# Zero rows of the short chunk on another engine, and the second pair's transposes and scores in other queues and banks

## The chip, the core and the metric

The kernel runs on one core of a Trainium2 chip. The metric is device time in microseconds, the median of several executions, and lower is better. One execution has been recorded by the hardware profiler, and all rows shown are from such recordings. The engines are TensorE (PE: matmuls; PEld: its weight loads), VectorE (DVE), ScalarE (ACT), GpSimd (POOL) and SyncE (SP, which issues nearly all transfers here). Each engine works through its own queue in program order. Matmuls write PSUM, which is divided into eight banks.

## The reference

Causal linear attention with a decay for each head ("retention"), followed by a gated feed-forward layer:

```python
# q, k, v: (8, 8, 576, 64) fp32
scores = (1 / sqrt(64)) * q @ k.T
gamma  = 1 - 2.0 ** (-5 - arange(8))                  # one for each head
D      = where(i >= j, gamma ** (i - j), 0)
x      = ((scores * D) @ v)                           # -> (4608 tokens, 512)
gate   = 1 / (1 + exp(-(x @ w_gate)))                 # w_gate, w_val: (512, 1536)
out    = (gate * (x @ w_val)) @ w_out                 # w_out: (1536, 512)
```

## The kernel before, in words

Each of the 8 sequences of 576 tokens is cut into chunks of 128, 128, 128, 128 and 64 tokens, which gives 45 steps; step 4 and step 9 are the short ones of 64 tokens ("short chunk") in the first two sequences. The decay is folded into q and k when they are cast to bf16 (tables qtab, ktab). Within a chunk the scores are masked by a triangle and multiplied with v; between chunks a state of k.T v is carried on for each head (PSUM tile "st", copied to "sbd" for each step). The attention's output goes, transposed, into xT. The feed-forward layer then takes blocks of tokens of xT: 12 GLU units (h: gate and value matmuls of 4 steps each, L567; a sigmoid on ACT; a product on VectorE) and the output matmuls ("op").

The order on every engine is written out by hand, in the order of the program text:

- The first four steps are done as two pairs (A = 0 and 1) of 256 tokens. For a pair, `cast_pair` casts and scales half of the heads of k, q or v (L232, v on ACT at L229), `pair_t` transposes half of k or q on TensorE into one PSUM bank and copies it out by the engine given (L297, L307), `pair_qk` makes half of the scores in two PSUM banks and masks them on VectorE (L316, L321), `pair_st` adds to the state (L330), `tile_sv` copies the state (L338), `pair_pv` makes the output (L352 from the state, L359 from the scores) and `pair_out` copies it to xT (L366).
- `fill(n)` issues n matmuls of zeros (L136) into a GLU bank; their result isn't used.
- `h_first(fcs, a, e)` runs GLU units of the first 512 tokens, for the given pieces of the hidden layer and columns. `cast_w` casts pieces of the GLU weights (L209), `cast_wo` those of the output weights (L214).
- Steps 4 to 9 run through `phase_tk`, `phase_tq`, `phase_qk`, `phase_st`, `phase_sv` and `phase_pv`, woven into the GLU and output matmuls of earlier tokens by `advance`. `run_phase("t", s)` first issues loads up to step s + 5 and casts up to step s + 2 (k, for later steps q, and v; on POOL). So when step 4 starts, POOL gets the casts of step 6 (L239, L258), which need the loads of step 6.
- In `phase_qk` a short chunk's scores fill 64 of the 128 partitions of tile "pte"; the other 64 are set to zero (L416), because `phase_pv` reads all 128 (L459).

PSUM banks by pool: "tr" 1, "qk" 2, "pv" 1, "st" 1, and "ffn" 3, which the GLU units, the fills, the output matmuls and some of the pairs' work share in turn. Loads go into 18 buffers, output rows into 4 ("osb"). The first output matmuls (L769) work on three blocks of 128 tokens at once and follow the product of step 4; the fourth block follows at L780.

Of the kernel before, what the change touches and what calls it, by code (L numbers as in the profile page):

```python
# [16 lines left out]
def kernel(  # L17
# [17 lines left out]
    nc = tc.nc  # L35
# [4 lines left out]
    P = 128  # L40
# [14 lines left out]
    tr_psum = ctx.enter_context(tc.tile_pool(name="tr_psum", bufs=1, space=PS))  # L55
    qk_psum = ctx.enter_context(tc.tile_pool(name="qk_psum", bufs=2, space=PS))
    pv_psum = ctx.enter_context(tc.tile_pool(name="pv_psum", bufs=1, space=PS))
    st_psum = ctx.enter_context(tc.tile_pool(name="st_psum", bufs=1, space=PS))
    ffn_psum = ctx.enter_context(tc.tile_pool(name="ffn_psum", bufs=3, space=PS))
# [71 lines left out]
    def fill(n):  # L131

        ps = ffn_psum.tile([P, 512], FP32, tag="ffn", name=f"idle_{fill.at}")
        fill.at += 1
        for i in range(n):
            nc.tensor.matmul(ps, lhsT=blank[:, 0:P], rhs=blank, start=True, stop=True)  # L136
# [69 lines left out]
    def cast_w(nm, f, nf, i, eng):  # L206
        r = NKC // nf
        at = (slice(None), slice(i * r, (i + 1) * r), slice(f * P, (f + nf) * P))
        eng(out=(wg_sb if nm == "g" else wv_sb)[at], in_=parts.pop((nm, f, i)))  # L209

    on_pool, on_act, on_dve = nc.gpsimd.tensor_copy, nc.scalar.copy, nc.vector.tensor_copy
# [75 lines left out]
    def half(x):  # L287
        return slice(x * 64, x * 64 + 64)
# [3 lines left out]
    def pair_t(nm, A, g, psum, tag, eng):  # L292
        ps = psum.tile([P, 2, 2, P], BF16, tag=tag, name=f"{nm}Tp_{A}_{g}")
        for i in range(2):
            for r in range(2):
                m = 2 * g + i
                nc.tensor.matmul(ps[:, i, r, :], lhsT=natural[nm, A][:, r, 2 * m:2 * m + 2, :], rhs=ident,  # L297
                                 is_transpose=True, start=(i == 0 and r == 0), stop=(i == 1 and r == 1))
        if nm == "k":
            if g == 0:  # L300
                turned["kp", A] = att_pool.tile([P, M, 2, P], BF16, tag="kp", name=f"kp_{A}", bufs=1)
            o = turned["kp", A][:, 2 * g:2 * g + 2]
        else:
            if g == 0:
                turned["qp", A] = att_pool.tile([P, M, 2 * P], BF16, tag="qp", name=f"qp_{A}", bufs=1)
            o = turned["qp", A][:, 2 * g:2 * g + 2, :].rearrange("p m (t r) -> p m r t", r=2)
        eng(out=o, in_=ps)  # L307

    def pair_qk(A, g, psum, tag):
        ps = [psum.tile([P, 2, 2, P], FP32, tag=tag, name=f"qkp_{A}_{g}_{hh}") for hh in range(2)]  # L310
        for i in range(2):
            m = 2 * g + i
            for r in range(2):
                for a in range(2):
                    for hh in range(2):
                        nc.tensor.matmul(ps[hh][half(a), i, r, :], lhsT=turned["kp", A][half(hh), m, r, half(a)],  # L316
                                         rhs=turned["qp", A][half(hh), m, a * P:(a + 1) * P], start=True, stop=True)
        if g == 0:
            probs["p", A] = att_pool.tile([P, 2, M, 2, P], BF16, tag="ptp", name=f"ptp_{A}", bufs=1)
        for hh in range(2):  # L320
            nc.vector.tensor_tensor(out=probs["p", A][:, hh, 2 * g:2 * g + 2], in0=ps[hh],  # L321
                                    in1=trip.unsqueeze(1).to_broadcast([P, 2, 2, P]), op=ALU.mult)
# [12 lines left out]
    def tile_sv(s, eng):  # L335
        sb = sbd[s % 3]
        for hh in range(2):
            eng(out=sb[half(hh), :, half(hh)], in_=st_tiles[STEPS[s][0]][half(hh)])  # L338
        state[s] = sb
# [3 lines left out]
    def pair_pv(A, g, a):  # L343
        s = 2 * A + a
        if g == 0:
            pair_ps[s] = (tr_psum if a else pv_psum).tile([P, M, P], FP32, tag="tr" if a else "pv", name=f"pvp_{s}")
        ps = pair_ps[s]
        if s > 0:
            for i in range(2):
                m = 2 * g + i  # L350
                for hh in range(2):
                    nc.tensor.matmul(ps[half(hh), m, :], lhsT=state[s - 1][:, m, half(hh)],  # L352
                                     rhs=turned["qp", A][:, m, a * P:(a + 1) * P],
                                     start=(m == 0), stop=False, skip_group_check=True)
        for i in range(2):
            m = 2 * g + i
            for r in range(2):
                for hh in range(2):
                    nc.tensor.matmul(ps[half(hh), m, :], lhsT=natural["v", A][half(a), r, 2 * m + hh, :],  # L359
                                     rhs=probs["p", A][half(a), hh, m, r, :],  # L360
                                     start=(s == 0 and m == 0 and r == 0), stop=(m == M - 1 and r == 1),
                                     skip_group_check=True)
# [39 lines left out]
    def phase_qk(s):  # L402
        b, c = STEPS[s]
        n = width[c]
        qT = turned["q", s]
        if s < EARLY:

            kT = turned["k", s]
            qkp = [qk_psum.tile([P, M, P], FP32, tag="qk", name=f"qk_{s}_{hh}") for hh in range(2)]
            for m in range(M):  # L410
                for hh in range(2):
                    nc.tensor.matmul(qkp[hh][0:n, m, 0:n], lhsT=kT[half(hh), m, 0:n], rhs=qT[half(hh), m, 0:n],
                                     start=True, stop=True)
            pt = att_pool.tile([P, 2, M, P], BF16, tag="pte", name=f"pte_{s}", bufs=2)
            if n < P:
                nc.gpsimd.memset(pt[n:P, :, :, 0:n], 0.0)  # L416
            for hh in range(2):
                nc.vector.tensor_tensor(out=pt[0:n, hh, :, 0:n], in0=qkp[hh][0:n, :, 0:n],
                                        in1=tri2[0:n, 0:n].unsqueeze(1).to_broadcast([n, M, n]), op=ALU.mult)
            probs[s] = pt  # L420
            return
        kb = turned["kb", s]
        pt = att_pool.tile([P, M, 192], BF16, tag="pt", name=f"pt_{s}")
        if n == P:
            for g in range(2):
                qkp = qk_psum.tile([P, 2, 256], FP32, tag="qk", name=f"qk_{s}_{g}")
                for mm in range(2):
                    m = 2 * g + mm
                    nc.tensor.matmul(qkp[:, mm, 0:128], lhsT=kb[:, 0, m, :], rhs=qT[:, m, 0:128],  # L429
                                     start=True, stop=True)  # L430
                    nc.tensor.matmul(qkp[:, mm, 128:192], lhsT=kb[:, 1, m, :], rhs=qT[:, m, 64:128],  # L431
                                     start=True, stop=True)
                nc.vector.tensor_tensor(out=pt[:, 2 * g:2 * g + 2, :], in0=qkp[:, :, 0:192],  # L433
                                        in1=tri.unsqueeze(1).to_broadcast([P, 2, 192]), op=ALU.mult)
        else:
            qkp = qk_psum.tile([P, 4, 128], FP32, tag="qk", name=f"qk_{s}")
            for m in range(M):
                nc.tensor.matmul(qkp[:, m, 0:64], lhsT=kb[:, 0, m, :], rhs=qT[:, m, 0:64],
                                 start=True, stop=True)
            nc.vector.tensor_tensor(out=pt[:, :, 0:64], in0=qkp[:, :, 0:64],  # L440
                                    in1=tri[:, 0:64].unsqueeze(1).to_broadcast([P, M, 64]), op=ALU.mult)
        probs[s] = pt
# [221 lines left out]
    def h_first(fcs, a, e):  # L664
        run(h_units(gvs, fcs, 0, a, e))
# [19 lines left out]
    pair_pv(0, 0, 0)  # L685
    fill(2)
    pair_pv(0, 0, 1)
    pair_pv(0, 1, 0)
    pair_out(0, 0, on_act)
    pair_pv(0, 1, 1)  # L690
    pair_out(0, 1, on_dve)
    pair_st(0, 1)
    for i in range(2):
        cast_w("g", 0, 2, i, on_pool)
    cast_w("v", 0, 2, 0, on_dve)
    cast_w("v", 0, 2, 1, on_act)
    cast_pair("k", 1, 0, nc.gpsimd)
    cast_pair("k", 1, 1, nc.gpsimd)
    tile_sv(1, on_dve)
    fill(4)  # L700

    h_first((0, 1), 0, 2 * P)
    cast_pair("q", 1, 0, nc.vector)
    pair_t("k", 1, 0, tr_psum, "tr", on_dve)
    cast_pair("q", 1, 1, nc.vector)
    pair_t("k", 1, 1, pv_psum, "pv", on_dve)
    fill(1)
    pair_t("q", 1, 0, tr_psum, "tr", on_act)
    pair_t("q", 1, 1, pv_psum, "pv", on_act)
    fill(3)  # L710
    pair_qk(1, 0, qk_psum, "qk")
    cast_pair("v", 1, 0, None)
    cast_pair("v", 1, 1, None)
    fill(4)
    pair_qk(1, 1, qk_psum, "qk")
    for i in range(2):
        cast_w("g", 2, 2, i, on_pool)
    pair_st(1, 0)
# [111 lines left out]
```

## Time and profile before

| | |
|---|---|
| median of 3 runs | 359.36 us (358.45 to 360.49) |
| the profiled execution | 359.63 us, span 357.9 us |
| granted TensorE clock, mean | 0.986 |
| PE, DVE, ACT, POOL busy | 338.4, 180.0, 127.8, 161.5 us |
| PE idle in the stage of the second pair (13.74 to 24.96 us) | 2.05 us |
| PE idle from 45.13 to 53.45 us | 8.32 us |

The span runs from the first to the last instruction; the execution's own time is somewhat longer. In rows of a timeline the columns are the start in microseconds, the duration, the engine, the line of the kernel, the operation, the tile written <- the tiles read, shapes, how many instructions are merged in the row (x), and in brackets the idle time of that engine before the row with what ended it. A matmul's duration includes its way through the array, so starts, not durations, tell the rate. "Waits" list who waited for whom.

### The profile page before, as it was taken

The numbers are of one execution on the slowest core, as the hardware profiler recorded it, in microseconds if no ns is written. First come the engines' busy times: TensorE is split into PE (matmuls) and PEld (weight loads), VectorE is DVE, ScalarE is ACT, GpSimd is POOL, SyncE is SP. The second block draws the span as 40 slices with busy tenths as digits, with TensorE's granted clock in tenths as the row PEclk, the third lists the DMA queues.
The fourth block names the chain that finished last, engine by engine and source line by source line (L and its number), as shares of the span: only waits on it lengthen the run. The fifth ranks groups of instructions, "written<-read, shape, count | busy, mean of one in ns | idle before, by whom it ended". The sixth has DMA issues, their size and how long they took to land.

```text
span 357.9 us, 7236 instructions
## 1 busy us (share of the span) xinstructions
PE 338.4 (95%) x2713; PEld 196.2 (55%) x2747; DVE 180.0 (50%) x367; ACT 127.8 (36%) x246; POOL 161.5 (45%) x266
## 2 busy tenths in 40 slices
PE   8799909999999999999999999999999999999996
PEld 3566404677685655655656664555555545544443
DVE  4754530569485673642654784544465445502420
ACT  6466401444334423324424423342333233333321
POOL 7642863258664773444545865455366500000000
PEclk9999967999999999999999999999999999999999
DMA  8999999929599979955957998975993320011002
GB/s 231 315 380 257 275 252 193 210 73 202 113 196 195 177 148 238 187 89 142 178 113 159 149 206 191 165 119 119 213 173 58 88 75 0 2 59 59 2 27 90
DMA packets 147506, 54.73 MB, mean 153 GB/s; under 512 B 130960, under 2 KB 139408, under 8 KB 147472
## 3 DMA queue, kind: packets, MB, share of 16 engines
q1 hardware_dynamic: 147328, 54.15, 73.1%
q8 instruction: 21, 0.34, 0.5%
q10 hardware_dynamic: 144, 0.13, 0.1%
q14 instruction: 13, 0.11, 0.1%
HBM read 37.75 MB, written 9.44 MB: 132 GB/s over the span
## 4 chain that ended last, share of the span: by engine, by line
PE 81%; DMA 11%; DVE 2%; POOL 2%; SPq 2%; issue 1%; ACT 1%; ACTq 0%; POOLq 0%
PE h L567 45%; PE op L630 22%; DMA k<-in_k_dram 6%; PE pv L471 4%; DMA wg<-in_moe_w_gate_dram 3%; PE op L769 3%; DMA k32p<-in_k_dram 2%; PE qk L429 2%; PE st L492 2%; POOL ks L239 1%; SPq L90 1%; PE qk L431 1%; SPq L101 1%; DVE kbd L397 1%; PE op L780 1%
## 5 line engine op out<-in xcount | busy, mean ns | idle before, releaser
L567 PE MATMUL h<-xT,wg_sb 128*128 128x512 bf16 (+3 forms) x587 | 117.5, 321 | 0.6
L567 PE MATMUL h<-xT,wv_sb 128*128 128x512 bf16 (+3 forms) x583 | 116.6, 321 | 0.3
L594 DVE TENSOR_TENSOR gv<-g,h 128x512 bf16<-128x512 bf16 (+1 forms) x104 | 65.1, 626 | 70.4 <-PE h L567 67.2
L590 ACT ACTIVATE g<-h 128x512 bf16<-128x512 f32 (+1 forms) x104 | 57.0, 548 | 99.8 <-PE h L567 80.9
L630 PE MATMUL op<-wo_sb,gv 128*128 128x512 bf16 x357 | 84.2, 379 | 0.7
L567 PEld LDWEIGHTS <-wg_sb 128*128 128x128 bf16 x592 | 52.9, 98 | 38.5 <-issue 0.4
L567 PEld LDWEIGHTS <-wv_sb 128*128 128x128 bf16 x592 | 52.2, 98 | 32.9 <-DVE wv_sb L209 0.4
L239 POOL TENSOR_TENSOR ks<-k,ktab 128x512 bf16<-128x512 f32 (+1 forms) x36 | 37.5, 1041 | 65.3 <-issue 22.2
L267 POOL CAST vbd<-v 64x256 bf16<-64x256 f32 x108 | 43.6, 404 | 45.3 <-PE pv L471 40.2
L630 PEld LDWEIGHTS <-gv 128*128 128x128 bf16 x372 | 34.9, 98 | 37.6
L433 DVE TENSOR_TENSOR pt<-qk,tri 128x384 bf16<-128x384 f32 x48 | 24.5, 552 | 36.1 <-PE qk L431 36.1
L602 ACT COPY ob<-op 128x512 f32<-128x512 f32 x35 | 20.3, 587 | 59.0 <-PE op L630 48.6
L249 POOL TENSOR_TENSOR qs<-q,qtab 128x512 bf16<-128x512 f32 (+1 forms) x30 | 31.5, 1051 | 0.0
L472 ACT CAST xT<-pv 128x512 bf16<-128x512 f32 (+1 forms) x36 | 19.4, 539 | 30.5 <-PE pv L471 18.8
L397 DVE COPY kbd<-kT 64x512 bf16<-64x512 bf16 (+1 forms) x60 | 27.6, 460 | 0.9
L258 POOL CAST vn<-v 128x512 bf16<-128x512 f32 (+1 forms) x36 | 24.1, 669 | 1.5 <-PE pv L459 1.5
L504 DVE TENSOR_TENSOR sb<-st,bdm 128x512 bf16<-128x512 f32 x24 | 16.5, 688 | 5.7 <-PE st L492 5.7
L580 ACT ACTIVATE g<-h 128x256 bf16<-128x256 f32 x32 | 12.3, 384 | 17.9 <-PE h L567 14.8
L471 PE MATMUL pv<-pt,vbd 128*128 128x128 bf16 (+1 forms) x216 | 17.3, 204 | 0.0
L471 PEld LDWEIGHTS <-vbd 128*128 128x128 bf16 x216 | 14.7, 98 | 3.4
L471 PE MATMUL pv<-qT,sb 128*128 128x128 bf16 (+1 forms) x96 | 13.8, 213 | 0.0
L582 DVE TENSOR_TENSOR gv<-g,h 128x256 bf16<-128x256 bf16 x20 | 8.4, 421 | 9.9 <-ACT g L580 9.6
(93 smaller groups left out, 242.2 us busy)
## 6 DMA issues: line engine op xcount, KB each, us to landing
out_dram<-ob SPq DMA_DIRECT2D x35, 256.0 KB, 2.2
v<-in_v_dram SPq DMA_DIRECT2D x28, 256.0 KB, 3.7
k<-in_k_dram SPq DMA_DIRECT2D x28, 256.0 KB, 4.3
q<-in_q_dram SPq DMA_DIRECT2D x28, 256.0 KB, 4.9
wg<-in_moe_w_gate_dram SPq DMA_DIRECT2D x12, 256.0 KB, 5.6
wv<-in_moe_w_val_dram SPq DMA_DIRECT2D x12, 256.0 KB, 5.6
wo<-in_moe_w_out_dram SPq DMA_DIRECT2D x12, 256.0 KB, 5.7
k32p<-in_k_dram SPq DMA_DIRECT2D x4, 256.0 KB, 4.9
```

What stands on the lines that cost most here:

```text
L239: nc.gpsimd.tensor_tensor(out=ks[0:n], in0=k32[0:n], in1=ktab[0:n, c, :].unsqueeze(2).to_broadcast([n, H, D]), op=ALU.mult)
L249: eng.tensor_tensor(out=qs[0:n], in0=q32[0:n], in1=qtab[0:n, c, :].unsqueeze(2).to_broadcast([n, H, D]), op=ALU.mult)
L258: nc.gpsimd.tensor_copy(out=vn[0:n], in_=v32[0:n])
L267: nc.gpsimd.tensor_copy(out=vb[hh * 64:hh * 64 + 64, j, :, hh * 64:hh * 64 + 64], in_=v32[j * 64:j * 64 + 64, hh::2, :])
L397: nc.vector.tensor_copy(out=kb[p0:p0 + 64, 0:nj, :, p0:p0 + 64].rearrange("p j m t -> p m j t"), in_=kT[p0:p0 + 64, 0:M, 0:n].rearrange("p ...
L433: nc.vector.tensor_tensor(out=pt[:, 2 * g:2 * g + 2, :], in0=qkp[:, :, 0:192], in1=tri.unsqueeze(1).to_broadcast([P, 2, 192]), op=ALU.mult)
L471: nc.tensor.matmul(pvp[:, m, a:e], lhsT=w, rhs=x, start=(i == 0), stop=(i == len(mm) - 1))
L567: nc.tensor.matmul(out, lhsT=w_sb[:, kc, fc * P:(fc + 1) * P], rhs=xT[:, kc, t0 + a:t0 + e], start=(kc == 0), stop=(kc == NKC - 1))
L590: nc.scalar.activation(out=g[:, 0:n], in_=h1[:, 0:n], func=AF.Sigmoid)
L594: nc.vector.tensor_tensor(out=gvs[some[0]][:, a:e], in0=g[:, 0:n], in1=h2[:, 0:n], op=ALU.mult)
L602: nc.scalar.copy(out=ob, in_=opp)
L630: nc.tensor.matmul(opp, lhsT=gvs[fc][:, nb * P:(nb + 1) * P], rhs=wo_sb[:, fc, :], start=(fc == 0), stop=(fc == NFC - 1))
```

## The change

Two parts. First, the zero rows of the short chunks' tile "pte" (steps 4 and 9) are written by VectorE instead of GpSimd. Second, in the stage of the second pair:

- the casts of the first pair of GLU weight pieces (gate on POOL, value on VectorE and ACT) are placed ahead of the last three products of the first pair instead of behind them
- the second state copy goes from VectorE to ACT
- the cast of the first half of the second pair's q is placed between the two first GLU units instead of behind them
- the four transposes of the second pair are all copied by ACT (k's halves were by VectorE), the first of q goes to a GLU bank, the second to the "tr" bank
- the second half of its scores goes to two GLU banks instead of the "qk" banks
- the fills around it go from 4, 1, 3, 4 to 3, 1, 2, 3 matmuls, the last group now behind the second scores instead of ahead of them

```diff
             if n < P:
-                nc.gpsimd.memset(pt[n:P, :, :, 0:n], 0.0)
+                nc.vector.memset(pt[n:P, :, :, 0:n], 0.0)
...
     pair_pv(0, 0, 1)
+    for i in range(2):
+        cast_w("g", 0, 2, i, on_pool)
+    cast_w("v", 0, 2, 0, on_dve)
+    cast_w("v", 0, 2, 1, on_act)
     pair_pv(0, 1, 0)
     pair_out(0, 0, on_act)
     pair_pv(0, 1, 1)
     pair_out(0, 1, on_dve)
     pair_st(0, 1)
-    for i in range(2):
-        cast_w("g", 0, 2, i, on_pool)
-    cast_w("v", 0, 2, 0, on_dve)
-    cast_w("v", 0, 2, 1, on_act)
     cast_pair("k", 1, 0, nc.gpsimd)
     cast_pair("k", 1, 1, nc.gpsimd)
-    tile_sv(1, on_dve)
-    fill(4)
-
-    h_first((0, 1), 0, 2 * P)
+    tile_sv(1, on_act)
+    fill(3)
+
+    h_first((0,), 0, 2 * P)
     cast_pair("q", 1, 0, nc.vector)
-    pair_t("k", 1, 0, tr_psum, "tr", on_dve)
+    h_first((1,), 0, 2 * P)
+    pair_t("k", 1, 0, tr_psum, "tr", on_act)
     cast_pair("q", 1, 1, nc.vector)
-    pair_t("k", 1, 1, pv_psum, "pv", on_dve)
+    pair_t("k", 1, 1, pv_psum, "pv", on_act)
+    pair_t("q", 1, 0, ffn_psum, "ffn", on_act)
     fill(1)
-    pair_t("q", 1, 0, tr_psum, "tr", on_act)
-    pair_t("q", 1, 1, pv_psum, "pv", on_act)
-    fill(3)
+    pair_t("q", 1, 1, tr_psum, "tr", on_act)
+    fill(2)
     pair_qk(1, 0, qk_psum, "qk")
     cast_pair("v", 1, 0, None)
     cast_pair("v", 1, 1, None)
-    fill(4)
-    pair_qk(1, 1, qk_psum, "qk")
+    pair_qk(1, 1, ffn_psum, "ffn")
+    fill(3)
```

## The prediction

> **What bounds the kernel now.** I read the page first, then the waits of PE, a table by stage, and the timelines of single engines. The page:
>
> ```profile
> span 357.9 us, 7236 instructions
> PE 338.4 (95%) x2713; PEld 196.2 (55%) x2747; DVE 180.0 (50%) x367; ACT 127.8 (36%) x246; POOL 161.5 (45%) x266
> PEclk9999967999999999999999999999999999999999
> ```
>
> TensorE is busy in 95% of the span, so a change pays only by PE's holes, by its slow stretch, or by matmuls left out. The granted clock falls in one place, slices 6 and 7 (each 8.95 us, so 44.7 to 62.6 us). PE's waits (microseconds, times, longest) name the biggest hole:
>
> ```profile
> PE pv L459 <- POOL pte L416: 8.3, 1, 8.3
> PE qTp L297 <- DVE kp L307: 1.8, 2, 1.2
> ```
>
> By stage, the columns being length and then busy time with instruction counts of PE, PEld, DVE, ACT and POOL, clock, DMA share, GB/s:
>
> ```profile
> 13.74:24.96 11.22, 9.17 (x154) 5.99 (x154) 6.96 (x15) 5.16 (x10) 5.24 (x8) 1.00 1.10 356
> 24.96:45.13 20.17, 20.07 (x134) 11.30 (x131) 10.41 (x22) 10.67 (x22) 10.68 (x16) 1.00 1.08 277
> 45.13:53.45 8.32, 0.00 (x1) 0.00 (x0) 3.21 (x6) 0.00 (x0) 5.28 (x9) 0.64 1.11 251
> 53.45:60.52 7.07, 7.02 (x37) 3.12 (x38) 0.00 (x0) 0.37 (x1) 3.19 (x4) 0.70 1.22 197
> ```
>
> So there are two places to look at: 8.32 us of nothing on PE, followed by 7 us at a granted clock of 0.70, and the second pair's stage, where PE idles 11.22 - 9.17 = 2.05 us. The first, on POOL and PE:
>
> ```profile
> 37.62 0.52 POOL L262 MEMSET vn<- 64x512 bf16 x1
> 48.79 0.62 POOL L214 CAST wo_sb<-wo 128x512 bf16<-128x512 f32 x1 [0.16 <-DMA wo<-in_moe_w_out_dram]
> 51.22 1.04 POOL L239 TENSOR_TENSOR ks<-k,ktab 128x512 bf16<-128x512 f32 x1 [1.81 <-DMA k<-in_k_dram]
> 52.88 0.52 POOL L416 MEMSET pte<- 64x512 bf16 x1
> 31.07 1.03 PE L567 MATMUL h<-xT,wv_sb 128*128 128x512 bf16 x4
> 39.71 1.03 PE L567 MATMUL h<-xT,wv_sb 128*128 128x512 bf16 x4
> 53.45 0.26 PE L459 MATMUL pv<-pte,vn 128*64 128x64 bf16 x2 [8.32 <-POOL pte L416]
> 53.96 6.56 PE L769 MATMUL op<-wo_sb,gv 128*128 128x512 bf16 x20
> 60.36 0.39 PE L373 MATMUL kTp<-ident,ks 128*128 128x128 bf16 x4
> ```
>
> The zero rows of step 4 take 0.52 us, but in POOL's order they stand behind the key cast of step 6, which waits for a load. PE is released 0.05 us after the memset ends (53.40), so the memset really is the last thing it waits for.
>
> **Term A, the wait: 8.32 us.** On VectorE the same memset stands right ahead of the two mask products of step 4, in the same queue. The other work of POOL that this product needs, the zero rows of v, ended at 38.14, and its two mask products ended at 44.4, so nothing else holds it at 45.13. The memset's price on VectorE isn't in the trace in this shape; the nearest rows are these:
>
> ```profile
> 46.45 2.11 DVE L772 MEMSET vbd<- 128x512 uint32 x4
> 2.95 0.82 DVE L168 MEMSET sbd<- 128x256 uint32 x3
> ```
>
> The size is 512 bf16 for each partition, between 0.27 (0.82 / 3, the same bytes) and 0.53 us (2.11 / 4, the same count of elements); I take 0.27, the same bytes. VectorE has about 0.7 us free after those products, so this costs 0 (at the upper end too); without that cover it would cost 0.27 to 0.53 each for steps 4 and 9. POOL gets back 2 x 0.52 us that nobody will miss.
>
> **Term B, the slow clock: 2.15 us.** At full speed matmuls of 512 columns start (39.71 - 31.07) / 40 = 0.216 us apart. From 54.03 (the chain's first op matmul) to 60.52 there are 21 of them (7 rounds of 3; one record is missing), 6.49 us where 21 x 0.216 = 4.54 would do: 1.95. The 16 small ones ahead of them took 0.58 us, and the same 16 of step 9, at full clock, 0.38: 0.20. No other idle time of PE after the first pair exceeds 1.20 us, and the clock stays at 1.00 there, so with the hole gone I expect the loss to go whole.
>
> **Term C, the second pair: 2.1 us.** The rows of PE, then ACT, then DVE:
>
> ```profile
> 13.74 0.60 PE L567 MATMUL h<-xT,wg_sb 128*128 128x256 bf16 x4
> 17.59 0.38 PE L297 MATMUL qTp<-ident,qp 128*128 128x128 bf16 x4 [1.20 <-DVE kp L307]
> 18.52 0.38 PE L297 MATMUL qTp<-ident,qp 128*128 128x128 bf16 x4 [0.55 <-DVE kp L307]
> 19.48 0.42 PE L316 MATMUL qkp<-qp,kp 64*64 64x128 bf16 x16
> 22.99 0.30 PE L352 MATMUL pvp<-qp,sbd 128*64 128x128 bf16 x4
> 24.96 0.61 PE L567 MATMUL h<-xT,wg_sb 128*128 128x256 bf16 x4
> 6.88 1.07 ACT L307 COPY kp<-kTp 128x512 bf16<-128x512 bf16 x2 [1.91 <-PE kTp L297]
> 15.76 0.38 ACT L580 ACTIVATE g<-h 128x256 bf16<-128x256 f32 x1 [0.49 <-PE h L567]
> 18.06 1.61 ACT L307 COPY qp<-qTp 128x512 bf16<-128x512 bf16 x2 [1.92 <-PE qTp L297]
> 19.53 1.13 ACT L229 CAST vp<-v32p 128x512 bf16<-128x512 f32 x2
> 21.98 0.76 ACT L338 CAST sbd<-st 64x256 bf16<-64x256 f32 x2 [1.32 <-PE st L330]
> 13.33 0.85 DVE L209 CAST wv_sb<-wv 128x512 bf16<-128x512 f32 x1
> 15.30 0.42 DVE L582 TENSOR_TENSOR gv<-g,h 128x256 bf16<-128x256 bf16 x1 [0.35 <-ACT g L580]
> 17.45 0.68 DVE L232 TENSOR_TENSOR qp<-q32p,qtab 128x512 bf16<-128x512 f32 x1
> 19.94 1.29 DVE L321 TENSOR_TENSOR ptp<-qkp,trip 128x512 bf16<-128x512 f32 x2 [1.48 <-PE qkp L316]
> ```
>
> I run the new order through these durations. One fill fewer starts the first GLU unit at 13.74 - 0.22 = 13.52. Its product follows 1.56 after, at 15.08 to 15.50. The first q cast, now between the two products, ends near 16.1 (0.69 with a little overlap), the second product at 16.5, the second q cast at 17.1, where it ended at 18.13. The second sigmoid ends at 15.76 + 0.38 - 0.22 = 15.92; ACT then copies both k halves in 1.07, to 17.0. These copies are dearer than VectorE's, but earlier. The first q transpose goes to a GLU bank at 16.15 and the second to the "tr" bank at 17.15, so the waits of 1.20 and 0.55 are replaced by waits for the q casts of about 0.45 each. ACT's q copies (1.61) run 17.0 to 18.6, the v casts (1.13) to 19.7, the state matmuls to 20.0, and the state copy (0.76) to 20.8; it ended at 22.74. Scores of the first half start at 17.85, of the second at 18.65 (GLU banks, so no wait for masks to free their own); the four mask products (2 x 1.29) end at 20.8. The product that reads the state, at 22.99 before, starts at 20.85: 2.1 earlier. From there to the GLU at 24.96 PE ran without a wait, and does so again. The fills left out (three, 0.65 us) lie inside this and aren't counted twice.
>
> What is moved: the casts of the first value weights go ahead of the copies of the first outputs on both queues. If their loads are late, ACT and DVE stand still with those copies behind them, and the GLU waits; they ran without waiting at 12.67 and 13.33, now they are asked for at about 11.4 and 11.65, which the trace can't show. The second state copy goes to ACT at 12.9, where ACT is free until 14.67. No transfer's order on SP changes. The bounds of C are 0 and 2.7 (all 2.05 of idle and the 0.65); I take 2.1 by the chain.
>
> ```profile
> 22.94 0.42 DVE L209 CAST wv_sb<-wv 128x512 bf16<-128x512 f32 x1
> ```
>
> The moved VectorE cast lies beside POOL's weight casts at 11.38 to 12.55. The row at 13.33, beside POOL's key cast, took 0.85, while the same cast at 22.94 took 0.42 with POOL casting too; either way it ends by 12.5, before the output copy's 12.72. The Trainium skill, "SBUF — State Buffer", section "Who interferes with whom", says that a VectorE cast in a two-port mode and a GpSimd instruction shut each other out of a shared port for a whole instruction, whoever starts first. By it the cast could start only when POOL pauses, which would be told in another term (a rival below); the 0.85 leans that way, the 0.42 against.
>
> **After the shift: what is late next.** In 24.96 to 45.13 PE has no slack to give, so its inputs must be there 2.1 earlier. The output weights' last cast ends at 49.41; with A, B, C its round would start at about 51.5. Keys of step 6 are cast by 52.26; their transposes move from 68.5 to about 55.9. These hold. One thing doesn't fit so well:
>
> ```profile
> 60.71 1.41 SPq L81 DMA_DIRECT2D q<-in_q_dram  x1
> 65.21 1.35 SPq L609 DMA_DIRECT2D out_dram<-ob  x3
> 77.93 0.59 ACT L602 COPY ob<-op 128x512 f32<-128x512 f32 x1 [2.16 <-PE op L630]
> DMA to landing us min/median/max: 1.7/2.2/4.1
> ```
>
> SP is busy with loads until 62.1, and those wait for transfers, not PE. The first output stores can go only then. The fifth output copy (77.93, now 65.4) reuses the buffer of the first, whose store lands at 62.1 + 0.4 + 1.7 to 4.1 = 64.2 to 66.6. So ACT may wait 0 to 1.2 us, with a sigmoid behind it; GLU banks hide part. I charge **D = 0.3**, and for the range 0 to 1.5 with the loads crowding.
>
> **Sum.** 8.32 + 2.15 + 2.1 - 0.3 = 12.3 us. The profiled execution took 359.63 (span 357.9, and 1.73 around it), 0.27 above the median of 359.36, so I predict 359.63 - 12.3 = 347.3, a little high rather than low for a median.
>
> **Rivals.**
> 1. The pair's stage gives nothing: the early casts wait for their loads, or the second weights hold the GLU at 24.96. Speaking for it: DMA is full there (share 1.10); against: C's waits are by engines, not loads. 359.63 - 8.32 - 2.15 = 349.2. Chance 0.17.
> 2. The hole comes back in part as waits for loads, because PE runs 12 us earlier into transfers that don't move. Candidates are q of step 6, whose issue ended at 48.35 and whose cast now comes at about 52.8, and the stores above. A wait of 2 to 4 us gives 349.3 to 351.3. For it: DMA share 1.11 and 1.22 at 45 to 60; against: the k of step 6 landed by 51.2. Chance 0.14.
> 3. The shut-out: the value weights' cast waits until POOL's gap at 12.55 and ends near 13.0 to 13.3, and the copy behind it (0.69) at 13.9 instead of 13.41. The GLU starts 0.5 later: 347.8. [...] Chance 0.06.
> 4. The change doesn't do what it says: PE still waits at this product for something else on POOL. For it: one wait can hide others; against: v's zero rows ended 15 us earlier. It gives about 357 (C alone). Chance 0.02.
> 5. Slower: q of step 6 lands so late that VectorE stands at its cast with masks and GLU products queued behind it. In the old order it was cast at 65.17 without a wait, so it decides against the change only if it landed near there, 17 us after its issue; 360 or more. Chance 0.01.
>
> My forecast has 0.60. The range: C at 2.7, D at 0 and the runs' scatter give 345.8; rival 2 at 3.7 us gives 351.0. A measurement of this kernel tells about 0.5% (1.8 us) from no change; only cases 4 and 5 can come near: faster 0.97, same 0.02, slower 0.01.
>
> **What would show it.** A: no wait at line 459 near 43, and the memset on VectorE in 0.27 to 0.53 us. B: PEclk at 9 in slices 6 and 7. C: GLU units after the second pair at about 22.9, state copies for it done by 20.8. D: an idle of ACT before the output copy near 65. The prediction is wrong if PE shows a wait over 1 us for a DMA between 40 and 75 us, or if the clock drops again.

## The result, and the profile after

The changed kernel takes 348.19 us (median of 4 runs, 347.38 to 349.89) where the kernel before takes 359.33 (358.45 to 360.49): a ratio of 0.9694, 95% interval 0.9649 to 0.9740. The forecast was 347.3, in a range of 345.8 to 351.0. The profiled execution took 348.36 us, 11.27 less than the one of before; 12.3 had been forecast.

From the page of the changed kernel:

```profile
span 346.6 us, 7262 instructions
PE 338.1 (98%) x2744; PEld 195.3 (56%) x2744; DVE 180.1 (52%) x365; ACT 129.2 (37%) x250; POOL 160.0 (46%) x264
PEclk9999999999999999999999999999999999999999
```

TensorE's recorded busy time is nearly as before (338.1 against 338.4), so most of what went is idle time. The sum can't show the slow stretch: matmuls at the low clock count as busy, and the profile of before lacks some matmul records (2713 matmuls beside 2747 weight loads; after, 2744 beside 2744). The granted clock no longer falls in any slice. The waits of PE (microseconds in total, times, longest):

```profile
PE qk L412 <- ACT qT L387: 1.5, 2, 1.3
PE idle L136 <- DVE blank L129: 1.3, 1, 1.3
PE qk L429 <- DVE kbd L397: 0.8, 1, 0.8
PE qTp L297 <- DVE qp L232: 0.5, 2, 0.3
```

The wait of 8.3 us at line 459 is gone, and so are those of the second pair for VectorE's k copies. The one at line 412, at most 0.2 us before, now heads the list with 1.3 us. The stages that answer to those shown of before (length, then busy time of PE, PEld, DVE, ACT, POOL, clock, DMA share, GB/s):

```profile
13.71:22.98 9.27, 8.70 (x154) 5.69 (x153) 4.91 (x10) 6.19 (x13) 3.06 (x6) 1.00 1.11 349
22.98:43.15 20.17, 20.12 (x133) 11.11 (x128) 11.35 (x22) 10.67 (x22) 10.57 (x17) 1.00 1.09 285
43.15:53.08 9.93, 9.93 (x85) 4.73 (x85) 5.90 (x12) 1.63 (x4) 7.11 (x10) 1.00 1.03 258
```

The second pair's stage has shrunk from 11.22 to 9.27 us, and from the product of step 4 on PE works without a gap. The timelines of DVE and PE show the memset and what follows it (from about line 690 on, the changed kernel's lines stand one further down, so L770 is the L769 of before):

```profile
42.05 0.27 DVE L416 MEMSET pte<- 64x256 uint32 x1
42.36 0.75 DVE L418 TENSOR_TENSOR pte<-qk,tri 64x256 bf16<-64x256 f32 x2
43.33 0.69 DVE L594 TENSOR_TENSOR gv<-g,h 128x512 bf16<-128x512 bf16 x1 [0.23 <-PE h L567]
43.53 4.80 PE L770 MATMUL op<-wo_sb,gv 128*128 128x512 bf16 x21
48.17 0.39 PE L373 MATMUL kTp<-ident,ks 128*128 128x128 bf16 x4
```

The memset takes 0.27 us, and VectorE is again waiting 0.23 us for PE soon after it, so it is hidden. The 21 output matmuls and what follows them to step 5's transposes take 48.17 - 43.53 = 4.64 us; before it was 60.36 - 53.96 = 6.40.

**Where the 11.3 us came from.** I compared the starts of the same instruction in both profiles:

| stretch | before | after | gain |
|---|---|---|---|
| first GLU work behind the second pair | 24.96 | 22.98 | 1.98 |
| from there to the product of step 4 | 19.95 | 20.17 | -0.22 |
| from that product to the first output matmul | 9.05 | 0.38 | 8.67 |
| from there to step 5's transposes | 6.40 | 4.64 | 1.76 |
| on to step 7's transposes (78.17, 65.98) | 17.81 | 17.81 | 0.00 |
| on to step 7's scores (79.46, 68.36) | 1.29 | 2.38 | -1.09 |
| on to step 8's scores (84.96, 73.51) | 5.50 | 5.15 | 0.35 |
| on to step 10's scores (98.12, 86.81) | 13.16 | 13.30 | -0.14 |

The sum is 11.31; the spans differ by 11.3. So nothing is gained or lost behind 87 us.

### The profile page after: what moved, and what is told of

It reads as the page before. It is cut to its first block, busy times and chain, and to the rows that moved or that the text cites. A ratio compares the mean times of both kernels' runs of the same rounds, so it can differ in the third digit from the quotient of the medians.

```text
span 346.6 us, 7262 instructions
## 1 busy us (share of the span) xinstructions
PE 338.1 (98%) x2744; PEld 195.3 (56%) x2744; DVE 180.1 (52%) x365; ACT 129.2 (37%) x250; POOL 160.0 (46%) x264
## 4 chain that ended last, share of the span: by engine, by line
PE 76%; DVE 2%; ACT 0%; issue 0%; ACTq 0%
PE h L567 44%; PE op L630 22%; PE pv L471 4%; PE qk L429 2%; PE st L492 2%; DVE kbd L397 1%; PE qk L431 1%; PE op L620 1%; DVE pte L418 0%; DVE qs L249 0%; DVE sbd L338 0%; DVE gv L585 0%; PE qk L438 0%; ACT g L580 0%; DVE sb L504 0%
## 5 line engine op out<-in xcount | busy, mean ns | idle before, releaser
L567 PE MATMUL h<-xT,wv_sb 128*128 128x512 bf16 (+3 forms) x592 | 118.0, 322 | 0.1
L630 PE MATMUL op<-wo_sb,gv 128*128 128x512 bf16 x372 | 85.6, 379 | 0.0
L267 POOL CAST vbd<-v 64x256 bf16<-64x256 f32 x108 | 42.9, 397 | 41.5 <-PE pv L471 36.3
L249 POOL TENSOR_TENSOR qs<-q,qtab 128x512 bf16<-128x512 f32 (+1 forms) x30 | 32.3, 1075 | 1.1 <-DMA qT<-qs 1.0
L580 ACT ACTIVATE g<-h 128x256 bf16<-128x256 f32 x32 | 12.3, 384 | 17.3 <-PE h L567 13.4
```

What stands on the lines that cost most here:

```text
L249: eng.tensor_tensor(out=qs[0:n], in0=q32[0:n], in1=qtab[0:n, c, :].unsqueeze(2).to_broadcast([n, H, D]), op=ALU.mult)
L267: nc.gpsimd.tensor_copy(out=vb[hh * 64:hh * 64 + 64, j, :, hh * 64:hh * 64 + 64], in_=v32[j * 64:j * 64 + 64, hh::2, :])
L567: nc.tensor.matmul(out, lhsT=w_sb[:, kc, fc * P:(fc + 1) * P], rhs=xT[:, kc, t0 + a:t0 + e], start=(kc == 0), stop=(kc == NKC - 1))
L630: nc.tensor.matmul(opp, lhsT=gvs[fc][:, nb * P:(nb + 1) * P], rhs=wo_sb[:, fc, :], start=(fc == 0), stop=(fc == NFC - 1))
```

## The experiments

Theory 1 is the forecast's own sum, with the loss at step 7 put down to an output buffer. The rivals are told with each run. The first stages start up to 1 us apart in different executions (the first GLU unit at 13.71 us in the changed kernel, at 14.67 in qk_banks), so stages are compared by their lengths.

**The first part alone, and the second alone.** Edit of memset_only: the kernel before with `nc.vector.memset(pt[n:P, :, :, 0:n], 0.0)`. Edit of pair_only: the changed kernel with `nc.gpsimd.memset` there.

> Only the first part of the change: the zero rows of the short chunks on VectorE, the second pair as before. Theory 1 (the gain is wait 8.32 + slow clock 2.15 + pair stage 2.0, less about 1.1 that a late output store gives back): no wait at line 459, clock 1.00, the GLU after the second pair still at 24.96 us, and the fifth output copy at about 67.5 us, which is just after the first store lands, so nothing is given back: profiled run 359.6 - 10.5 = 349.2 us, median 348.7 to 349.5. Rival (the second part is worth its whole 2.0 us on top): 350.2 us. Rival (the second part is worth nothing): 348.2 us.

Measured: 349.6 us (349.1 to 349.83), ratio 0.972 (0.9696 to 0.9743); the profiled run 349.83. From its windows and ACT's timeline:

```profile
14.24:25.53 11.29, 9.24 (x154) 5.98 (x153) 7.25 (x15) 5.16 (x10) 5.16 (x8) 1.00 1.08 358
68.06 0.59 ACT L602 COPY ob<-op 128x512 f32<-128x512 f32 x1 [2.16 <-PE op L630]
```

This is theory 1 at its upper edge: the pair's stage keeps its length (11.29), the clock is 0.999, and the fifth output copy waits for PE only, so no output store gives anything back. The median is 0.1 above what I had written, and the rival at 350.2 isn't excluded by the time alone; what speaks is that the copy doesn't wait for a store. Nor do the times tell the second part's share of the whole gain: the ratios without and with it, 0.972 and 0.9694, have intervals that overlap. The stage's length shows it, 11.29 us here against 9.27.

> Only the second part of the change: the second pair's new order, the zero rows still on GpSimd. Theory 1: TensorE comes to the product of step 4 about 1.8 us earlier and waits there about 10.1 us instead of 8.3, until the same 53.4 us, because the memset stands behind a cast that waits for a load: 359.3 us, within 0.6 of before. Rival (the two parts simply add): 357.4 us.

Measured: 359.3 us (358.3 to 361.42), ratio 0.9993 (0.9971 to 1.0014). PE and POOL in it:

```profile
13.71:22.98 9.27, 8.65 (x152) 5.69 (x153) 4.91 (x10) 6.29 (x13) 3.74 (x6) 1.00 1.11 346
52.90 0.52 POOL L416 MEMSET pte<- 64x512 bf16 x1
53.48 0.27 PE L459 MATMUL pv<-pte,vn 128*64 128x64 bf16 x2 [9.96 <-POOL pte L416]
```

The pair's stage is as short as in the changed kernel (9.27), and PE then waits 9.96 us instead of 8.32 for the same memset, which ends at 53.42 as it did at 53.40 before. The whole 2 us of the second part are lost in front of a release that hangs on a load. The parts don't add; the second shows its 2 us only with the first.

**The clock by itself.** In before_fill PE is kept busy in the hole: the kernel before with `fill(36)` behind `h_first((11,), 0, 4 * P)`.

> The kernel before with 36 matmuls of zeros (7.8 us at full rate) put ahead of the product of step 4, into the hole. Theory 1 (the low clock comes from the hole itself): the product still starts at about 53.4 us, the clock stays at 1.00 and the output matmuls start 0.216 us apart from the first: 359.35 - 2.15 = 357.2 us, 357.0 to 357.6. Rival (the clock falls for another reason, the traffic or the kind of work): 359.4 us, clock under 0.8 in slices 6 and 7 as before.

Measured: 357.6 us (356.74 to 358.44), ratio 0.9946 (0.9926 to 0.9966). Its windows of the hole and of what follows, and PE's timeline:

```profile
45.00:53.50 8.50, 7.74 (x37) 3.39 (x37) 3.21 (x6) 0.00 (x0) 5.76 (x9) 1.00 1.12 258
53.50:60.50 7.00, 6.95 (x56) 3.53 (x56) 0.42 (x1) 0.96 (x2) 2.78 (x4) 1.00 1.05 200
53.50 0.22 PE L459 MATMUL pv<-pte,vn 128*64 128x64 bf16 x2 [0.71 <-POOL pte L416]
53.84 4.71 PE L770 MATMUL op<-wo_sb,gv 128*128 128x512 bf16 x21
```

The product still starts at 53.50, held by the same memset, and useless matmuls ahead of it are worth 2.17 us, because the 21 output matmuls behind it run at a granted clock of 1.00 (4.71 us instead of 6.56). Term B is shown, at its size: the slow clock belongs to the idle time and not to the traffic, which was the same (258 and 200 GB/s in the two windows, against 251 and 197 before).

**Engine or place in the queue.** In pool_early the memset of step 4 is back on POOL, at the head of `run_phase("t", 4)`:

```diff
+            if s == 4:
+                n = width[STEPS[s][1]]
+                zeroed[s] = att_pool.tile([P, 2, M, P], BF16, tag="pte", name=f"pte_{s}", bufs=2)
+                nc.gpsimd.memset(zeroed[s][n:P, :, :, 0:n], 0.0)
             while done["cast"] < min(NS, s + LEAD_CAST + 1):
```

> The changed kernel, but the zero rows of step 4 are written by GpSimd again, now ahead of the casts of step 6 in its queue (those of step 9 by GpSimd in the old place). Theory 1 (the place in the queue is what counted): no wait at line 459, 348.2 us, 347.6 to 348.8. Rival (the engine counted: GpSimd is too slow or too late there): a wait of 1 us or more at line 459, 350 us or more.

Measured: 356.43 us (355.25 to 357.48), ratio 0.9914 (0.9885 to 0.9942). My expectation missed by 8 us. POOL and PE show why:

```profile
49.63 0.61 POOL L214 CAST wo_sb<-wo 128x512 bf16<-128x512 f32 x1 [0.16 <-DMA wo<-in_moe_w_out_dram]
50.31 0.52 POOL L536 MEMSET pte<- 64x512 bf16 x1
50.88 0.26 PE L463 MATMUL pv<-pte,vn 128*64 128x64 bf16 x2 [7.35 <-POOL pte L536]
```

It now stands ahead of step 6's cast, but twelve casts of output weights, which the program issues earlier, were still ahead of it, the last of them landing near 49.6. I had looked at the one instruction ahead of the memset and not at the queue: past step 6's casts the memset is only 2.6 us earlier. PE is released 0.05 us after the memset again, and the time follows: 50.88 instead of pair_only's 53.48, and 2.9 us less by the medians. pool_front moves it ahead of these as well, behind `cast_v(4)`:

```diff
     cast_v(4)
+    n4 = width[STEPS[4][1]]
+    zeroed[4] = att_pool.tile([P, 2, M, P], BF16, tag="pte", name="pte_4", bufs=2)
+    nc.gpsimd.memset(zeroed[4][n4:P, :, :, 0:n4], 0.0)
```

> The changed kernel with the zero rows of step 4 on GpSimd, now right behind the casts of step 4 and so ahead of the casts of the output weights, of step 5 and of step 6 (pool_early had moved it ahead of step 6's alone, and it then ended with the last cast of the output weights at 50.83 us). Theory 1 (place in the queue, not engine): the memset ends near 39 us, no wait at line 459, 347.9 us, 347.3 to 348.6. Rival (on GpSimd it costs more even when it is early, because 0.52 us delay the output weights' casts behind it): TensorE waits at the output matmuls of the first 512 tokens, 349 us or more.

Measured: 347.92 us (346.98 to 351.01), ratio 0.9691 (0.9628 to 0.9755), no wait at the product:

```profile
38.78 0.52 POOL L743 MEMSET pte<- 64x512 bf16 x1
43.70 4.81 PE L777 MATMUL op<-wo_sb,gv 128*128 128x512 bf16 x21
```

On POOL at 38.78 it is as good as on VectorE. So the first part of the change acts by the place in the queue; the engine and the 0.25 us between 0.52 and 0.27 don't matter here.

**What the new wait is.** The changed kernel's SP, ACT and PE around 60 to 68 us:

```profile
60.72 1.69 SPq L81 DMA_DIRECT2D q<-in_q_dram  x1
62.50 2.51 SPq L609 DMA_DIRECT2D out_dram<-ob  x3
63.20 0.38 ACT L580 ACTIVATE g<-h 128x256 bf16<-128x256 f32 x1 [0.46 <-PE h L567]
67.23 0.59 ACT L602 COPY ob<-op 128x512 f32<-128x512 f32 x1 [3.65 <-DMA out_dram<-ob]
67.72 0.59 ACT L387 COPY qT<-qTp 128x512 bf16<-128x512 bf16 x1
68.36 0.40 PE L412 MATMUL qk<-qT,kT 64*128 64x128 bf16 x8 [1.32 <-ACT qT L387]
```

ACT's fifth output copy waits 3.65 us for a store (its releaser); the q copy of step 7 stands behind it, and PE's scores wait for that. Three runs bear on it, each an edit of the changed kernel: osb5 (`bufs=5` for "osb"), store_act (the first three stores issued by `nc.scalar.dma_start`), and osb3 (`bufs=3`), with the changed kernel itself beside them.

> The changed kernel again, beside the next three on one chip: 348.2 us, 347.8 to 348.6, TensorE waiting 1.3 us at line 412 near 67 us.

> The changed kernel with five buffers for output rows instead of four. Theory 1 (the wait of 1.3 us near 67 us is the fifth output copy waiting on ScalarE for the first store, whose buffer it takes): ScalarE doesn't wait 3.65 us there, TensorE's wait at line 412 is about 0.2, and the time is 1.1 us less than the changed kernel's: 347.1 us. Rival (the wait belongs to the late cast or transposes of step 7): TensorE still waits about 1.3 us, 348.2 us.

> The changed kernel with four buffers, the first three output stores issued by ScalarE instead of SyncE. Theory 1 (the store is late because SyncE's queue holds it behind loads until 62.5 us): they are issued by about 55 us and land by about 60, ScalarE's wait is gone, 347.1 to 347.5 us (ScalarE pays about 0.4 us for each issue at a time when it has room). Rival (the transfers themselves are too crowded): the stores land as late as before, 348.2 us.

> The changed kernel with three buffers for output rows. Theory 1: the fourth output copy (55.9 us) has to wait for the first store to land at about 67 us, ScalarE stands for 11 us and TensorE for about 9 to 10 with it, and then the clock falls for some 4 us: 358 to 361 us, the whole gain lost. Rival (output buffers don't matter here): 348.2 us.

| | median (range), us | ratio to before | fifth output copy of ACT: its wait | PE's longest wait at L412 |
|---|---|---|---|---|
| after_again | 347.92 (347.53 to 348.24) | 0.9679 (0.9663 to 0.9695) | 3.15, for a store | 0.81 |
| osb5 | 346.47 (346.17 to 348.27) | 0.9661 (0.9633 to 0.9688) | 2.16, for PE | 0.23 |
| store_act | 347.25 (346.77 to 347.36) | 0.9658 (0.9644 to 0.9673) | 2.16, for PE | 0.23 |
| osb3 | 358.70 (one run) | | (fourth: 12.15, for a store) | 9.66 |

The first store of store_act, the rows of the copy in osb5 and in osb3, then PE in osb3:

```profile
53.63 0.38 ACTq L609 DMA_DIRECT2D out_dram<-ob  x1
65.33 0.58 ACT L602 COPY ob<-op 128x512 f32<-128x512 f32 x1 [2.16 <-PE op L630]
67.06 0.59 ACT L602 COPY ob<-op 128x512 f32<-128x512 f32 x1 [12.15 <-DMA out_dram<-ob]
68.19 0.61 PE L412 MATMUL qk<-qT,kT 64*128 64x128 bf16 x8 [9.66 <-ACT qT L387]
PEclk9999999599999999999999999999999999999999
```

With one more buffer, or with the first three stores taken out of SyncE's queue, the copy waits for PE alone and the wait at line 412 falls to 0.23, its size before. With one buffer less the copy that waits is the fourth, PE stands 9.66 us, the clock falls behind it (to 5 in one slice), and the gain is nearly all gone: 358.70. So the wait is the output buffer's, and it is late because its store stands behind loads in SyncE's queue until 62. In store_act the three stores took as long to land as in the changed kernel, 3.7 to 4.7 us against 3.6 to 4.7, so the transfers are as slow as the rival had them; but they were issued from 53.63 to 56.32 and had landed by 61.0. By the times the two better versions aren't told apart from the changed kernel with certainty: the intervals overlap. By its median osb5 is the fastest kernel run here, by its ratio store_act; that the wait of 0.6 to 1.1 us more than 0.23 is gone is shown by the traces.

**What shortens the pair's stage.** qk_banks puts the second half of the scores back in the qk banks (`pair_qk(1, 1, qk_psum, "qk")`); k_dve puts both k copies back on VectorE (`on_dve`).

> The changed kernel with the second half of the second pair's scores back in the two qk banks, nothing else. Theory 1 (the banks are what gains in the pair's stage): these scores wait for the masks of the first half, at about 19.1 and 19.7 us instead of 18.3, the state copy and all behind it come about 1.2 us later, and the GLU after the pair starts at 24.1 us instead of 22.98. Rival (the earlier q casts and copies are what gains, the banks don't matter): GLU at 23.0 to 23.2 us.

> The changed kernel with the copies of the second pair's k transposes back on VectorE, nothing else. Theory 1: VectorE does a copy in 0.42 us where ScalarE takes 0.53, but its queue then delays the second q cast by about 0.4 us, so that the GLU after the pair starts at 23.0 to 23.4 us: worth 0 to 0.4. Rival (the copies on ScalarE carry the pair's gain): GLU at 24 us or later.

Measured: 349.57 and 348.97 us, one run each, so their times decide nothing. The stage, from the first GLU unit to the GLU behind the pair, for qk_banks, k_dve, and the scores in qk_banks:

```profile
14.67:25.29 10.62, 8.94 (x154) 5.75 (x153) 5.17 (x10) 6.23 (x13) 5.07 (x8) 1.00 1.06 343
13.89:23.49 9.60, 8.70 (x153) 5.68 (x153) 5.67 (x12) 5.42 (x11) 3.23 (x5) 1.00 1.08 333
20.14 0.24 PE L316 MATMUL qkp<-qp,kp 64*64 64x128 bf16 x1 [0.79 <-DVE ptp L321]
20.73 0.41 PE L316 MATMUL qkp<-qp,kp 64*64 64x128 bf16 x15 [0.36 <-DVE ptp L321]
```

The stage takes 9.27 us in the changed kernel, 10.62 with the old banks and 9.60 with the k copies on VectorE. The banks are worth 1.35 of the 1.95 us, against 1.1 expected, because the scores wait for the masks of the first half to free their banks (0.79 and 0.36). The engine of the k copies is worth 0.33, inside the 0 to 0.4 expected. Each was taken back alone and once, so the two needn't add up. How the rest divides between the earlier q cast, the placement of the weight casts and the fills wasn't tried.

## Why the prediction was right, and by how much it was off

- **Term A, 8.32 us: right.** The kind of cause was right (a queue, not a slow engine), and the memset's price of 0.27 too. But the prediction named only step 6's key cast as what stood ahead; pool_early shows that of the wait only 2.6 us hang on step 6, and the rest on the casts of the output weights and of step 5 ahead of them. It made no difference here, because the change leaves POOL's queue altogether. From the product of step 4 to step 5's transposes, A and B together were forecast at 10.47 and measured 8.67 + 1.76 = 10.43.
- **Term B, 2.15 us: right.** before_fill measures it alone: 2.17 by the medians. Its part of 0.20 rests on a miscount: of the 16 small matmuls two ran at 44.91, ahead of the wait. For the other 14 the timeline gives 53.96 - 53.45 = 0.51 against 43.53 - 43.20 = 0.33 in the changed kernel, so 0.18, and 0.18 + 1.76 = 1.94 for the whole term in that trace.
- **Term C, 2.1 us: 1.98, right.** The chain's steps came out close: scores of the first half at 17.97 (17.85 written), the GLU at 22.98 (22.86). The first unit started at 13.71 and not at 13.52; the first pair's work ran 0.15 later in this execution. The q transposes wait 0.21 and 0.32 for the q casts, where 0.45 was written. ACT's q copies took 1.48 and not 1.61, but no row of PE in this stage waits for ACT: the product that reads the state starts at 21.00 behind two fills, with the state copy done at 20.76. So the path through ACT that the prediction followed to 20.85 ended just ahead of PE's own work, and that the two agree so well is in part luck. The loads that the trace of before couldn't answer for were nearly in time: ACT's early weight cast waited 0.32 us for its load (at 11.86), and the GLU didn't wait for it.
- **"In 24.96 to 45.13 PE has no slack to give": this step missed 0.22.** I checked that inputs landed, not that casts got slower. In the changed kernel VectorE's casts of value weights for the fifth GLU unit moved in beside POOL's gate weight casts (27.59 to 30.36). The last two rows are of before:

```profile
28.31 0.84 DVE L209 CAST wv_sb<-wv 128x512 bf16<-128x512 f32 x1
27.59 2.77 POOL L209 CAST wg_sb<-wg 128x512 bf16<-128x512 f32 x4 [2.73 <-DMA wg<-in_moe_w_gate_dram]
29.09 1.25 PE L567 MATMUL h<-xT,wv_sb 128*128 128x512 bf16 x4
30.29 0.42 DVE L209 CAST wv_sb<-wv 128x512 bf16<-128x512 f32 x1
27.00 2.65 POOL L209 CAST wg_sb<-wg 128x512 bf16<-128x512 f32 x4 [2.61 <-DMA wg<-in_moe_w_gate_dram]
```

  The cast took 0.84 instead of 0.42, and the unit's value matmuls 1.25 instead of 1.03. Before, these casts came behind POOL's (30.29 against an end of 29.65). That is rival 3's mechanism at another place than the one where I priced it. At its own place the cast took 0.63 and ended at 12.35, ahead of the copy at 12.87 that it could have held up, so the rival fell there; it didn't wait out POOL's two casts, which ran until 12.82. The Trainium skill, "SBUF — State Buffer", section "Who interferes with whom", says that a VectorE instruction in a two-port mode, which a cast can enter, and a GpSimd instruction lock each other out of a shared port for a whole instruction. The 0.84 beside POOL agrees with it; that the wait always lasts a whole instruction of the other engine isn't shown, since after_again has one such cast at 0.42 and the next at 0.86.
- **Term D, 0.3 us: the term that was mis-sized.** The mechanism was named (fifth output copy, buffer of the first, store behind loads on SyncE), but it cost 1.09 us at step 7's scores. The first store was issued at 62.50 (62.1 written) and landed 4.7 us later, at 67.2, where 64.2 to 66.6 was written. In the rows that the prediction read, a store took at most 4.1 us to land, counted from its issue. The output matmuls were done at 65.7, so the copy ran 1.5 late, and 1.09 of that passed to PE (1.32 at line 412 against 0.23 in the row of before, below), more than I had thought the GLU banks would let through. 0.35 came back at step 8, where a wait of 0.45 for VectorE's q cast had vanished.

```profile
79.46 0.40 PE L412 MATMUL qk<-qT,kT 64*128 64x128 bf16 x8 [0.23 <-ACT qT L387]
```

- The sum missed by 1.0 us: D 0.58 net of the small changes behind it, 0.22 for the casts, 0.12 for C, and rounding.
- Rival 1 (the pair gives nothing) fell by the stage's 9.27 us, though pair_only shows it true where the first part is missing. Rival 2 (the hole comes back in part as waits for transfers) fell at its size of 2 to 4 us, and no wait of PE was for a load. But the stores were among its candidates, and PE's 1.32 us at 68.36 hang on one, through ACT. So the sign of being wrong that the prediction gave, a wait of PE over 1 us for a DMA between 40 and 75 us, is absent only by the letter. Rival 4 fell by the row of the product, which starts without a wait, and rival 5 by VectorE's q cast of step 6, which ran at 52.98 without one.

## What to carry to other kernels

A cheap instruction that an engine reaches late costs as much as what stands ahead of it in that queue: list the whole queue back to the last wait, since moving it past one waiting instruction only finds the next. An idle hole on TensorE costs more than its length, because the granted clock falls behind it (here 8.32 us of idling cost 2.17 more, by before_fill), and what is gained ahead of such a hole is lost in it. When an engine is moved 12 us ahead of transfers that don't move, look at what is reused first (output buffers here) and at which stores stand behind loads in one queue.

## What was not expected of the hardware

- Matmuls of zeros in an otherwise idle stretch of 8.3 us made the kernel 2.17 us faster (before_fill; 2.15 had been worked out beforehand), with the release of the work behind them unchanged.
- In the changed kernel a store of 256 KB took 4.7 us from its issue to landing where the DMA share is 1.08 (62.50 to 67.20), against 2.0 to 2.1 us from 300 us on, where it is 0.10, and a median of 2.2 us for all output stores. That the other transfers are the reason wasn't tried.
